# A fused attention and two-layer feed-forward kernel: layer 1 in three passes over 512 tokens

## The chip, the cores and the metric

The kernel runs on one core of one Trainium2 chip. The metric is device microseconds of one execution. The core's engines are named as in the profile: PE (TensorE, matmuls) and PEld (its weight loads), DVE (VectorE), ACT (ScalarE), POOL (GpSimd), SP (SyncE, which issues most DMAs); a q behind a name is that engine's sequencer.

## The reference, cut to what matters

```python
# q, k, v: (batch 2, heads 8, seq 768, 64); each query attends to the keys with its own 6-bit hash
q_bits = (q @ proj > 0); k_bits = (k @ proj > 0)         # bucket = the six bits
scores = where(q_bucket == k_bucket, q @ k.T / 8, -1e9)
attn = softmax(scores) @ v                               # -> x, 1536 tokens x 512
g = x @ w_gate                                           # layer 1: 512 -> 1536 -> 512
x = (g * sigmoid(g) * (x @ w_val)) @ w_out
h = x @ w_in                                             # layer 2: 512 -> 2048 -> 512
out = (max(h, 0) + alpha * min(h, 0)) @ w_out2
```

## The kernel before, in words

All matmul operands are split in two rounded parts, high and low, and each product is made of three matmuls (high by high, high by low, low by high; `mm3`). The engines' queues run in order; a scheduler lays the program out, and instructions that are pinned keep the program's order.

**Attention** goes item by item: 24 items, each a pair of heads and 256 queries, for batch 0 then 1, and per batch the 256-token groups in order with four pairs in each. An item has two units (heads); a unit makes three banks of scores, takes the maximum over the keys (VectorE, tiles `m`), broadcasts it by transposes, subtracts it (`se`, L303), takes the exponent and multiplies with the values (`po`, L315). K and Q come from DRAM; of K three copies are fetched at an item that is the first of its pair and batch: the two heads one above the other (`nat`), and side by side into the two halves of `kt` (L160, L161). The generator `attention` yields 16 times per item; the caller advances it with `more()`.

**Layer 1** has 12 feature blocks f of 128. For each, `gate` and `value` products (4 x 3 matmuls each) go into PSUM, then tanh (ScalarE), two gate steps (VectorE, L587 and L590), the high part (ScalarE) and the low part (GpSimd, L602); three blocks later (`D1`) the output product of the block is added into four accumulators that stay in PSUM (`Y`). `stage1(g)` does this for 256 tokens, where a PSUM bank holds two gate products of 256 columns; `stage1w` for 512. Groups 0 to 3 (tokens 0 to 1023) are run by `stage1`, woven with attention: after each `yield` of `stage1` the caller makes `RATES[g]` steps of attention. Group g starts when its four items are done, so four items run alone first. The last 512 tokens are run by `stage1w` after attention has ended.

**Weights** are blocks of 128 x 512, 36 for layer 1. They come as 64-bit words: a raw block is loaded (L488, two buffers), `round64` turns it into float32 (ACT L505, DVE L506 and L508, POOL L510), and it is split into the high part (ACT L545) and the low part (L552, by turns on GpSimd and VectorE) in a buffer `wb`, of which there are six. The first time a block is used its split form is also written to DRAM (`w`, L556); every later pass reloads it from there (L500). `w_ahead` says how many blocks ahead of the one in use loads, conversions and splits are issued (`LEAD`). Of layer 2's 32 blocks, 12 are converted beside groups 2 and 3 and parked in DRAM (`EARLY`, `whole`), 20 beside `stage1w` (`w_late`: two raw loads per feature block, issued on SP's queue ahead of the reloads).

**Layer 2** (`stage2`) runs three times over 512 tokens. X, layer 1's input and output, lies in SBUF whole (`xh`, `xl`), and is overwritten in place.

## Time and profile before

| | us |
|---|---|
| median of 3 runs (908.02 to 909.84) | 909.22 |
| the profiled execution, first to last instruction (its span) | 907.9 |
| PE busy by overlapping durations | 842.3 (93%) |
| DVE busy | 563.6 (62%) |
| ACT busy | 440.4 (49%) |
| POOL busy | 374.8 (41%) |

The profile is of one execution. Busy times are unions of durations, and matmul durations overlap, so PE's share overstates it; the time of a matmul in a full stream is the distance of starts. A share over the whole span mixes stages with different limits: the rows further below are therefore cut by stage.

### The profile page before, as it was taken

Reading aid. Unit: us, or ns where it says so; the run is one execution under the profiler, and the core shown is the slowest. Engines: PE = TensorE matmul, PEld = TensorE weight load, DVE = VectorE, ACT = ScalarE, POOL = GpSimd, SP = SyncE. Lnnn points to the kernel's source line nnn. Section 1 sums busy time; section 2 is a strip of 40 time slices with the busy share of each in tenths; the row PEclk is TensorE's granted clock in tenths of the full one; section 3 lists DMA queues with packets and bytes.
Section 4 is the critical chain, followed back from the end, with each engine's and each line's share of the span. In section 5 each row is a group of like instructions: output and inputs, shape, how many; then the busy total and the mean of one; then the engine's idle time right before and its main releaser. Section 6 shows DMA issues by size and latency. Waiting matters only on the chain.

```text
span 907.9 us, 13038 instructions
## 1 busy us (share of the span) xinstructions
PE 842.3 (93%) x4816; PEld 736.4 (81%) x4816; DVE 563.6 (62%) x856; ACT 440.4 (49%) x760; POOL 374.8 (41%) x327
## 2 busy tenths in 40 slices
PE   4797878777999999999999999899999999999998
PEld 3576776666899999999999987788888888888886
DVE  5699998978777657678786537563433343335332
ACT  5687565655655656565655323222433343333331
POOL 4214666665443312233221235454444444445442
PEclk8899998988999999999999999999999999999999
DMA  9324776788999756766766698998100010000001
GB/s 219 85 81 162 240 243 214 225 262 247 332 344 272 225 191 215 252 231 220 252 217 213 224 330 309 342 338 303 46 1 1 1 47 0 1 12 36 1 0 47
DMA packets 63487, 158.45 MB, mean 175 GB/s; under 512 B 18112, under 2 KB 24256, under 8 KB 63424
## 3 DMA queue, kind: packets, MB, share of 16 engines
q1 hardware_dynamic: 61264, 152.07, 50.6%
q0 software_dynamic: 2016, 5.51, 2.8%
q8 instruction: 38, 0.62, 0.3%
q14 instruction: 25, 0.20, 0.1%
q10 hardware_dynamic: 144, 0.05, 0.0%
HBM read 132.44 MB, written 25.17 MB: 174 GB/s over the span
## 4 chain that ended last, share of the span: by engine, by line
PE 67%; DVE 15%; DMA 4%; POOL 3%; issue 2%; ACT 2%; SPq 0%; DVEq 0%; POOLq 0%; ACTq 0%
PE po L315 9%; PE gp L607 5%; PE gp L609 5%; PE gp L608 5%; PE op L612 5%; PE hp L607 5%; PE hp L608 5%; PE op L613 5%; PE op L614 5%; PE hp L609 5%; PE yp L607 3%; PE yp L609 3%; PE yp L608 3%; DVE wt L508 2%; DMA raw<-in_wblk_dram 2%
## 5 line engine op out<-in xcount | busy, mean ns | idle before, releaser
L602 POOL TENSOR_TENSOR gl<-ex,gh 128x512 fp32r<-128x512 f32 (+1 forms) x108 | 117.1, 1084 | 293.2 <-ACT gh L599 242.6
L607 PE MATMUL gp<-xh,wb 128*128 128x256 f32 (+1 forms) x480 | 154.4, 322 | 11.9 <-ACT wb L545 5.9
L609 PE MATMUL gp<-xh,wb 128*128 128x256 f32 (+1 forms) x480 | 148.8, 310 | 6.9 <-POOL wb L552 5.5
L315 PE MATMUL po<-se,vv 128*128 128x256 f32 x576 | 146.2, 391 | 3.9 <-ACT se L308 3.3
L608 PE MATMUL gp<-xl,wb 128*128 128x256 f32 (+1 forms) x480 | 147.3, 307 | 2.6 <-POOL xl L344 2.6
L593 DVE TENSOR_SCALAR ex<-hp,al 128x512 f32<-128x512 f32 x48 | 36.0, 751 | 137.8 <-PE hp L609 137.8
L315 PEld LDWEIGHTS po<-se,vv 128*128 128x128 f32 x576 | 106.3, 197 | 17.8 <-ACT se L308 5.0
L599 ACT ACTIVATE gh<-ex 128x512 fp32r<-128x512 f32 (+1 forms) x108 | 57.8, 535 | 125.7 <-DVE ex L596 66.8
L545 ACT ACTIVATE wb<-w 128x512 fp32r<-128x512 f32 x96 | 60.6, 632 | 101.1 <-PE hp L609 79.2
L607 PEld LDWEIGHTS gp<-xh,wb 128*128 128x128 f32 x480 | 91.8, 191 | 21.7 <-ACT wb L545 9.0
L609 PEld LDWEIGHTS gp<-xh,wb 128*128 128x128 f32 x480 | 92.3, 192 | 13.1 <-POOL wb L552 7.1
L608 PEld LDWEIGHTS gp<-xl,wb 128*128 128x128 f32 x480 | 92.2, 192 | 7.1 <-POOL xl L344 2.8
L308 ACT ACTIVATE se<-se 128x1536 f32<-128x1536 f32 x48 | 71.3, 1485 | 51.8 <-DVE se L303 51.6
L303 DVE SCALAR_TENSOR_TENSOR se<-se,mb 128x1536 f32<-128x1536 f32 x48 | 83.8, 1745 | 7.8 <-PE mb L298 7.5
L278 ACT ACTIVATE se<-S 128x512 f32<-128x512 f32 x144 | 80.0, 594 | 17.4 <-PE S L277 16.0
L510 POOL TENSOR_TENSOR wt<-wt,wr 128x512 int32<-128x512 int32 x48 | 67.6, 1410 | 49.4 <-DVE wt L508 31.3
L276 PE MATMUL S<-QA,kt 128*128 128x256 f32 x288 | 81.1, 310 | 2.9 <-ACT se L278 1.4
L607 PE MATMUL yp<-gh,wb 128*128 128x256 f32 (+1 forms) x240 | 78.1, 327 | 4.2 <-ACT wb L545 4.1
L609 PE MATMUL yp<-gh,wb 128*128 128x256 f32 (+1 forms) x240 | 73.7, 313 | 4.5 <-POOL wb L552 4.5
L277 PE MATMUL S<-qb,kt 76*128 76x256 f32 x288 | 74.0, 288 | 2.2 <-ACT kt L199 2.1
L607 PE MATMUL hp<-xh,wb 128*128 128x512 f32 x192 | 74.7, 389 | 0.0
L608 PE MATMUL hp<-xl,wb 128*128 128x512 f32 x192 | 74.7, 389 | 0.0
(94 smaller groups left out, 1839.2 us busy)
## 6 DMA issues: line engine op xcount, KB each, us to landing
wb<-w SPq DMA_DIRECT2D x144, 512.0 KB, 4.6
raw<-in_wblk_dram SPq DMA_DIRECT2D x68, 512.0 KB, 4.4
w<-wb SPq DMA_DIRECT2D x36, 512.0 KB, 5.1
qr<-in_q_dram SPq DMA_DIRECT2D x24, 256.0 KB, 3.9
kt<-in_k_dram POOLq DMA_DIRECT2D x14, 384.0 KB, 9.4
nat<-in_k_dram SPq DMA_DIRECT2D x8, 384.0 KB, 6.8
vv<-in_v_dram SPq DMA_DIRECT2D x16, 192.0 KB, 7.0
whole<-wt SPq DMA_DIRECT2D x12, 256.0 KB, 2.2
```

Of the source, the lines that this page charges most:

```text
L276: nc.tensor.matmul(pt[:, i, :], lhsT=ka[:, sl], rhs=qa, start=True, stop=False)
L277: nc.tensor.matmul(pt[:, i, :], lhsT=kb[:, sl], rhs=qb, start=False, stop=True)
L278: nc.scalar.activation(out=u.se[:, 2 * j:2 * j + 2, :], in_=pt, func=AF.Copy)
L303: nc.vector.scalar_tensor_tensor(out=u.se, in0=u.se, scalar=FLOOR, in1=u.mx[:, None, :].to_broadcast([P, NC, GQ]), op0=ALU.max, op1=ALU.su ...
L308: nc.scalar.activation(out=u.se, in_=u.se, func=AF.Exp, scale=SCALE)
L315: nc.tensor.matmul(it.po[:, u.x, :], lhsT=VV[it.b, it.p][:, kb, u.x * D:u.x * D + P], rhs=u.se[:, kb, :], start=kb == 0, stop=kb == NC - 1)
L510: pin(nc.gpsimd.tensor_tensor(out=a, in0=a, in1=r, op=ALU.add))
L545: nc.scalar.activation(out=w_tile(i)[:, 0, :], in_=wt[i], func=AF.Copy)
L602: nc.gpsimd.tensor_tensor(out=l, in0=ex, in1=f32(h), op=ALU.subtract)
L607: nc.tensor.matmul(pt, lhsT=h, rhs=ah, start=first, stop=False)
L608: nc.tensor.matmul(pt, lhsT=h, rhs=al_, start=False, stop=False)
L609: nc.tensor.matmul(pt, lhsT=l, rhs=ah, start=False, stop=last)
```

## The change

Layer 1 runs three times over 512 tokens (chunks 0, 1, 2), all by the same generator. Chunk 0 starts when its eight items are done; chunks 0 and 1 are woven with attention at 1.9 steps per yield, chunk 2 runs alone with the late conversions. The output product is no longer accumulated over all blocks in PSUM: after blocks 0-3, 4-7 and 8-11 (`QF` = 4; issued one block later) a `quad` makes the four output blocks, each 12 matmuls into a bank of the gate products' tags, and copies or adds it to `acc` in SBUF. For this an output weight block holds 4 feature blocks of one output block, and its raw load reads four pieces. X is a ring of two chunks: chunk 0's result is written to DRAM and read back before its layer-2 pass, which is the last (order 1, 2, 0). `wb` has four buffers in layer 1 and six of its own in layer 2, with shorter leads in layer 1. K is fetched twice instead of three times; the second half of `kt` is copied by ScalarE. The prefetch of the first raw blocks begins at step 64 of attention, not 32; all 12 early blocks are converted beside chunk 1. The final low parts of chunks 0 and 1 are made by GpSimd.

```diff
-NGB = 2
-NEX = 3
+NG1 = 5
+NEX = (2, 3)
...
-WB = (3, 6)
-LEAD = (3, 4, 5, 7)
+WB = (3, 4, 6)
+LEAD = ((2, 2, 3, 5), (3, 4, 5, 7))
...
-D1 = 3
+QF = 4
...
-PRIME = (32, 6)
-RATES = (2.0, 2.4, 2.6, 2.6)
-EARLY = (0, 0, 6, 6)
+PRIME = (64, 6)
+RATES = (1.9, 1.9)
+EARLY = (0, 12)
+AHEAD = 6
...
-        return XG(it.b * NG + it.g, it.p)
+        c, i = divmod(it.b * NG + it.g, W // GQ)
+        return [t[:, it.p, i * GQ:(i + 1) * GQ] for t in chunk(c)]
...
-        nc.gpsimd.dma_start(out=KB(it)[0:D], in_=kview(it))
...
+    def copy_k(it, x):
+        nc.scalar.activation(out=KB(it)[0:D, x, :], in_=f32(KA(it))[0:D, x, :], func=AF.Copy)
...
+            todo += [lambda x=x: copy_k(it, x) for x in range(2)]
...
-        u.m1 = at.sm.tile([P, GQ], F32, tag="m1", name="m1", bufs=1)
+        u.m1 = m2[:, 0, :]
...
+    def quad_at(f):
+        return f // QF - 1 if f % QF == 0 and f else None
...
-        for f in range(F1 + D1):
-            if f < F1:
-                o += [2 * f, 2 * f + 1]
-            if f >= D1:
-                o.append(F1O + f - D1)
-        return o
+        for f in range(F1):
+            o += [2 * f, 2 * f + 1]
+            q = quad_at(f)
+            o += [] if q is None else range(F1O + q * KD, F1O + (q + 1) * KD)
+        return o + list(range(F2I - KD, F2I))
...
-    seq = order1() * (len(RATES) + 1) + o2 * NP2
+    seq = order1() * NP2 + o2 * NP2
     NWT = len(seq)
+    NW1 = NWT - len(o2) * NP2
...
-        ready[i] = wp.tile([P, 2, 512], F32R, tag="wb", name="wb", bufs=WB[1])
+        if i < NW1:
+            ready[i] = wp.tile([P, 2, 512], F32R, tag="wb", name="wb", bufs=WB[1])
+        else:
+            ready[i] = fin.pool.tile([P, 2, 512], F32R, tag="wb2", name="wb2", bufs=WB[2])
...
-        pin(nc.sync.dma_start(out=t, in_=wblk[w].bitcast(I32).rearrange("p (f t) -> p f t", t=2)))
+        if F1O <= w < F2I:
+            q, e = divmod(w - F1O, KD)
+            src = wblk[F1O + q * QF:F1O + (q + 1) * QF, :, e * P:(e + 1) * P].bitcast(I32)
+            pin(nc.sync.dma_start(out=t.rearrange("p (f c) t -> p f (c t)", f=QF),
+                                  in_=src.rearrange("f p c -> p f c")))
+        else:
+            pin(nc.sync.dma_start(out=t, in_=wblk[w].bitcast(I32).rearrange("p (f t) -> p f t", t=2)))
...
+        lead = LEAD[n >= NW1]
         for name, k, fn in (("load", 2, w_load), ("conv", 1, w_conv), ("h", 0, w_h)):
-            upto(name, n + LEAD[0] + k, fn)
-        upto("l", n + LEAD[0], w_l)
-        upto("h", n + LEAD[1], w_h)
+            upto(name, n + lead[0] + k, fn)
+        upto("l", n + lead[0], w_l)
+        upto("h", n + lead[1], w_h)
         upto("put", n + 1, w_put)
-        upto("conv", n + LEAD[2], w_conv)
-        while ws.load < min(NWT, n + (LEAD[3] if fresh[min(ws.load, NWT - 1)] else LEAD[2])):
+        upto("conv", n + lead[2], w_conv)
+        while ws.load < min(NWT, n + (lead[3] if fresh[min(ws.load, NWT - 1)] else lead[2])):
...
+    def gate_bank(tag):
+        return at.ps.tile([P, W], F32, tag=tag, name="gp", bufs=at.nb[tag])
+    def quad(q, acc, gs, xh, xl):
+        for e in range(KD):
+            h, l = flat(w_next())
+            yp = gate_bank("GY"[e % 2])
+            for i in range(QF):
+                sl = slice(i * P, (i + 1) * P)
+                mm3(yp, (h[:, sl], l[:, sl]), *gs[q * QF + i], i == 0, i == QF - 1)
+                if i == 1:
+                    yield
+            if q == 0:
+                nc.scalar.activation(out=acc[:, e, :], in_=yp, func=AF.Copy)
+            else:
+                nc.vector.tensor_tensor(out=acc[:, e, :], in0=yp, in1=acc[:, e, :], op=ALU.add)
+            if q == F1 // QF - 1:
+                nc.scalar.activation(out=xh[:, e, :], in_=acc[:, e, :], func=AF.Copy)
+                eng = nc.gpsimd if ws.busy else nc.vector
+                eng.tensor_tensor(out=xl[:, e, :], in0=acc[:, e, :], in1=f32(xh)[:, e, :], op=ALU.subtract)
+            yield
+    def stage1(c, conv=()):
+        xh, xl = chunk(c)
+        acc = at.lt.tile([P, KD, W], F32, tag="acc", name="acc", bufs=1)
...
+        conv = iter(conv)
...
+            ps = []
+            ex = tmp()
+            for tag in "GY":
+                pt = gate_bank(tag)
+                w = w_next()
+                for kk in range(KD):
+                    mm3(pt, (w[0][:, kk, :], w[1][:, kk, :]), xh[:, kk, :], xl[:, kk, :], kk == 0, kk == KD - 1)
+                    if kk == 1:
+                        yield
+                if tag == "G":
+                    gate_tanh(pt, ex)
+                    gate_mul(pt, ex)
+                    yield
+            gs[f] = g_tiles()
+            gate_val(pt, ex)
+            split_h(gs[f][0], ex)
+            split_l(gs[f][0], gs[f][1], ex)
+            yield
+            q = quad_at(f)
+            if q is not None:
+                yield from quad(q, acc, gs, xh, xl)
+        yield from quad(F1 // QF - 1, acc, gs, xh, xl)
...
         for i in range(W // P):
-            out_rows(t0 + i * P, ops[i], i, tmp())
+            out_rows(t0 + i * P, ops[i], i, fin.pool.tile([P, W], F32, tag="ob", name="ob", bufs=4))
...
-    X = [tx.tile([P, KD, B * S], F32R, name=n) for n in ("xh", "xl")]
+    CH = {}
+    def chunk(c):
+        if c not in CH:
+            CH[c] = [tx.tile([P, KD, W], F32R, tag=n, name=n, bufs=2) for n in ("xh", "xl")]
+        return CH[c]
...
-    while at.done < NPAIR:
-        at.alone = at.done < NPAIR - 2
+    per = NPAIR * (W // GQ)
+    while at.done < per:
+        at.alone = at.done < per - 2
...
-    for g, rate in enumerate(RATES):
-        while at.done < NPAIR * (g + 1):
-            more()
+    ws.busy = True
+    spill = dram.tile([2, P, KD * W], F32, name="spill")
+    for c, rate in enumerate(RATES):
         due = 0.0
         pre = 0.0
-        for _ in stage1(g):
-            pre += EARLY[g] / F1
+        over = 0
+        for _ in stage1(c):
+            pre += EARLY[c] / 20
...
-                more()
+                over += at.done >= per * (c + 2)
+                if over <= AHEAD:
+                    more()
+        while at.done < per * (c + 2):
+            more()
+        if c == 0:
+            for i, t in enumerate(chunk(0)):
+                nc.sync.dma_start(out=spill[i], in_=f32(t).rearrange("p k w -> p (k w)"))
...
-    stage1w(len(RATES) * GQ)
-    for n in range(NP2):
-        stage2(n * W)
+    ws.busy = False
+    for _ in stage1(2, w_late()):
+        pass
+    for n, c in enumerate((1, 2, 0)):
+        if n == 1:
+            CH.pop(0)
+            for i, t in enumerate(chunk(0)):
+                nc.sync.dma_start(out=f32(t).rearrange("p k w -> p (k w)"), in_=spill[i])
+        stage2(c)
```

Three places show how instructions move. On VectorE, in the stage that converts the 36 blocks, before (group 0; `raw` is a raw block, `m` a maximum, `ex<-ex,gp` a gate step):

```order
L506 TENSOR_SCALAR wt<-raw_1528 128x512
L552 TENSOR_TENSOR wb<-wt,wb 128x512
L508 SCALAR_TENSOR_TENSOR wt<-raw_1528,wt 128x512
L303 SCALAR_TENSOR_TENSOR se<-se,mb 128x1536
L506 TENSOR_SCALAR wt<-raw_1573 128x512
L285 TENSOR_TENSOR m_1922<-m_1919 128x256
L508 SCALAR_TENSOR_TENSOR wt<-raw_1573,wt 128x512
L506 TENSOR_SCALAR wt<-raw_1615 128x512
L587 SCALAR_TENSOR_TENSOR ex<-ex,gp 128x256
L508 SCALAR_TENSOR_TENSOR wt<-raw_1615,wt 128x512
L552 TENSOR_TENSOR wb<-wt,wb 128x512
L590 SCALAR_TENSOR_TENSOR ex<-ex,gp 128x256
```

In the changed kernel (chunk 0):

```order
L299 TENSOR_REDUCE mq<-mt 128x2
L571 TENSOR_TENSOR wb<-wt,wb 128x512
L198 TENSOR_SCALAR mk<-hp,ck 44x384
L288 TENSOR_TENSOR m_2421<-se 128x512
L525 TENSOR_SCALAR wt<-raw_2413 128x512
L309 SCALAR_TENSOR_TENSOR se<-se,mb 128x1536
L289 SCALAR_TENSOR_TENSOR m_2421<-se,m_2421 128x512
L527 SCALAR_TENSOR_TENSOR wt<-raw_2413,wt 128x512
L291 TENSOR_TENSOR m_2421<-m_2421 128x256
L607 SCALAR_TENSOR_TENSOR ex<-ex,gp 128x512
L198 TENSOR_SCALAR mk<-hp,cq 44x256
L525 TENSOR_SCALAR wt<-raw_2466 128x512
```

Before, the rounding steps of three blocks and one subtraction stand around the two gate steps of a feature block; now one block's steps and the first of another's, a whole maximum and a subtraction stand around a gate step of twice the width.

On PE, in the woven stage, before (`S` are scores, `mt` and `mb` the transposes of the maximum):

```order
L607 MATMUL yp<-gh,wb 128x256
L608 MATMUL yp<-gl,wb 128x256
L609 MATMUL yp<-gh,wb 128x256
L276 MATMUL S<-QA,kt_127 128x256
L277 MATMUL S<-qb_67,kt_127 128x256
L276 MATMUL S<-QA,kt_127 128x256
L277 MATMUL S<-qb_67,kt_127 128x256
L291 MATMUL mt<-ident,m_4127 128x128 x2
L298 MATMUL mb<-ident,mq 128x128 x2
L607 MATMUL gp<-xh,wb 128x256
L608 MATMUL gp<-xl,wb 128x256
L609 MATMUL gp<-xh,wb 128x256
```

In the changed kernel, in chunk 0:

```order
L282 MATMUL S<-QA,kt_124 128x256
L283 MATMUL S<-qb_66,kt_124 128x256
L627 MATMUL gp<-xh,wb 128x512
L628 MATMUL gp<-xl,wb 128x512
L629 MATMUL gp<-xh,wb 128x512
L627 MATMUL gp<-xh,wb 128x512
L628 MATMUL gp<-xl,wb 128x512
L629 MATMUL gp<-xh,wb 128x512
L297 MATMUL mt<-ident,m_3003 128x128 x2
L304 MATMUL mb<-ident,mq 128x128 x2
L627 MATMUL gp<-xh,wb 128x512
L628 MATMUL gp<-xl,wb 128x512
```

Attention's instructions are the same; the matmuls of layer 1 between them stream 512 columns, and stand in runs of six, as a yield follows two of the four k blocks.

On SP's queue, in the last pass of layer 1, where raw blocks of layer 2 are loaded beside reloads, before:

```order
L488 DMA raw_6119<-in_wblk_dram 128x1024
L488 DMA raw_6126<-in_wblk_dram 128x1024
L500 DMA wb<-w_83 128x1024
L500 DMA wb<-w_98 128x1024
L500 DMA wb<-w_84 128x1024
L488 DMA raw_6185<-in_wblk_dram 128x1024
L488 DMA raw_6192<-in_wblk_dram 128x1024
L500 DMA wb<-w_85 128x1024
L500 DMA wb<-w_99 128x1024
L500 DMA wb<-w_86 128x1024
```

In the changed kernel:

```order
L507 DMA raw_5024<-in_wblk_dram 128x1024
L507 DMA raw_5031<-in_wblk_dram 128x1024
L519 DMA wb<-w_86 128x1024
L519 DMA wb<-w_87 128x1024
L507 DMA raw_5076<-in_wblk_dram 128x1024
L507 DMA raw_5083<-in_wblk_dram 128x1024
L519 DMA wb<-w_88 128x1024
L519 DMA wb<-w_89 128x1024
L507 DMA raw_5128<-in_wblk_dram 128x1024
L507 DMA raw_5135<-in_wblk_dram 128x1024
```

Two raw loads are now followed by two reloads instead of three, while the output product's four reloads stand together elsewhere.

## Rows read from the trace of the kernel before

**Rows 1.** Busy time by stretch: engine busy us (instructions), PE clock, DMA share, GB/s.

```profile
0.00:86.00 86.00, 63.13 (x334) 49.59 (x334) 65.52 (x103) 59.06 (x101) 28.55 (x36) 0.92 0.54 129
86.00:239.50 153.50, 121.93 (x729) 106.12 (x730) 134.17 (x190) 89.85 (x161) 94.47 (x77) 0.91 0.78 250
239.50:540.60 301.10, 297.16 (x2173) 283.66 (x2171) 207.12 (x345) 168.27 (x302) 84.92 (x86) 1.00 0.75 245
540.60:642.70 102.10, 98.83 (x433) 80.94 (x434) 56.80 (x70) 31.69 (x52) 48.56 (x36) 1.00 0.86 312
642.70:907.90 265.20, 261.25 (x1153) 216.07 (x1151) 100.04 (x151) 91.50 (x147) 118.25 (x93) 1.00 0.03 13
```

**Rows 2.** Waits of PE, 86 to 239.5: us in total, times, longest.

```profile
PE gp L607 <- ACT wb L545: 5.9, 10, 0.9
PE gp L609 <- POOL wb L552: 5.5, 6, 1.6
```

**Rows 3.** Waits of all engines, 86 to 239.5.

```profile
ACT wb L545 <- POOL wt L510: 34.2, 21, 3.3
POOL wt L510 <- DVE wt L508: 23.8, 19, 3.7
```

**Rows 4.** Lines of DVE, 100.4 to 239.5: busy us, mean ns; idle before.

```profile
L508 DVE SCALAR_TENSOR_TENSOR wt<-raw,wt 128x512 int32<-128x512 int32 x30 | 27.1, 902 | 0.1
L506 DVE TENSOR_SCALAR wt<-raw 128x512 int32<-128x512 int32 x29 | 22.1, 763 | 1.3 <-DMA raw<-in_wblk_dram 1.3
L303 DVE SCALAR_TENSOR_TENSOR se<-se,mb 128x1536 f32<-128x1536 f32 x10 | 17.5, 1747 | 2.6 <-PE mb L298 2.5
L552 DVE TENSOR_TENSOR wb<-wt,wb 128x512 fp32r<-128x512 f32 x16 | 14.2, 885 | 7.6 <-ACT wb L545 7.4
L283 DVE SCALAR_TENSOR_TENSOR m<-se,m 128x512 f32<-128x512 f32 x9 | 9.8, 1091 | 0.2
L282 DVE TENSOR_TENSOR m<-se 128x512 f32<-128x512 f32 x9 | 8.5, 948 | 3.7 <-ACT se L278 3.7
L285 DVE TENSOR_TENSOR m<-m 128x256 f32<-128x256 f32 x10 | 7.1, 712 | 0.0
...
L590 DVE SCALAR_TENSOR_TENSOR ex<-ex,gp 128x256 f32<-128x256 f32 x12 | 4.9, 410 | 0.1
```

**Rows 5.** Single lines of DVE, whole span: ns min/median/max, first and last start.

```profile
L506 DVE TENSOR_SCALAR wt<-raw x48: 377/433/2337, 68.9 to 539.2; 128x512 int32<-128x512 int32 x48
...
L587 DVE SCALAR_TENSOR_TENSOR ex<-ex,gp x60: 402/421/689, 100.4 to 630.0; 128x256 f32<-128x256 f32 x48, 128x512 f32<-128x512 f32 x12
...
L282 DVE TENSOR_TENSOR m<-se x48: 648/692/1770, 17.1 to 497.1; 128x512 f32<-128x512 f32 x48
```

**Rows 6.** Timeline of PE, 256 columns: start us, duration us.

```profile
386.12 0.28 PE L607 MATMUL yp<-gh,wb 128*128 128x256 f32 x1
386.24 0.28 PE L608 MATMUL yp<-gl,wb 128*128 128x256 f32 x1
```

**Rows 7.** Timeline of PE, 512 columns.

```profile
700.25 0.39 PE L609 MATMUL hp<-xh,wb 128*128 128x512 f32 x1
700.47 0.39 PE L607 MATMUL hp<-xh,wb 128*128 128x512 f32 x1
```

**Rows 8.** Chain that ended last: start us, us; half an item's value products.

```profile
353.95 2.59 PE po L315 x12
```

**Rows 9.** Timeline of SP's queue, 540 to 578.

```profile
549.79 2.37 SPq L488 DMA_DIRECT2D raw<-in_wblk_dram  x2
...
555.34 2.78 SPq L488 DMA_DIRECT2D raw<-in_wblk_dram  x2
...
562.51 2.36 SPq L488 DMA_DIRECT2D raw<-in_wblk_dram  x2
```

**Rows 10.** Waits of PE, whole span.

```profile
PE gp L607 <- DMA wb<-w: 4.7, 3, 2.7
...
PE gp L607 <- DVE ex L590: 0.2, 1, 0.2
```

**Rows 11.** DMA issues, the page's part 6: KB each, median us to landing.

```profile
wb<-w SPq DMA_DIRECT2D x144, 512.0 KB, 4.6
```

More of the change, by code (lines that the diff above doesn't have):

```diff
@@ L624, in out_rows @@
         nc.sync.dma_start(out=out[r0:r0 + P, :], in_=ob)
-    gbank = []
-    def half_bank():
-        if not gbank:
-            t = at.ps.tile([P, 2, GQ], F32, tag="G", name="gp", bufs=2)
-            gbank.extend(((t[:, 1, :], 1), (t[:, 0, :], 0)))
-        return gbank.pop()
-    def full(w, xh, xl):
-        pt, n = half_bank()
-        for kk in range(KD):
-            mm3(pt, (w[0][:, kk, :], w[1][:, kk, :]), xh[:, kk, :], xl[:, kk, :], n == 0 and kk == 0,
-                n == 1 and kk == KD - 1)
-        return pt
@@ L726, in stage2 @@
                 ex = tmp()
-                gs[f] = [fin.pool.tile([P, W], F32R, tag=t, name=t, bufs=D2 + 1) for t in ("gh2", "gl2")]
+                gs[f] = g_tiles()
                 leak(hp, f, ex)
```

79 lines of the change are left out of this document (10 added, 69 removed).

## The prediction

> **What bounds the kernel now.** I began with the table of stretches [rows 1], cut where layer 1 changes its token group. Layer 2 (642.7 to the end) and the wide pass before it keep TensorE busy without a gap. So do groups 1 to 3 of layer 1, together 301.1 us with attention in between. Time is lost in two places: the first 86 us, where attention runs alone, and group 0 (86.0 to 239.5), where TensorE works 121.93 of 153.5 us by the overlapping durations, at a granted clock of 0.91 of 2.4 GHz. The waits of group 0 come next. TensorE waits for the high part of a weight from ScalarE and the low part from GpSimd [rows 2], and these wait further back in the conversion, ScalarE 34.2 us for GpSimd's rounding sum [rows 3], which itself follows VectorE's two rounding steps. VectorE is 134.17 us busy there, 87%: a group of 256 tokens has too little matmul work to lie beside the conversion of all 36 weight blocks.
>
> The lines of VectorE from the first gate multiply (100.4) to 239.5 show how full it is [rows 4, 5]. These rows sum to 111 us; the other gate step (5.0) and some 42 small operations at about 0.41 us bring it to some 133 of 139.1 us, 96%. A rounding step takes 0.763 us in the mean there, 0.433 in the median over the kernel, 2.337 at the longest [rows 4, 5].
>
> **TensorE's prices.** Only starts count, as durations overlap. In full streams a 256-column matmul starts 0.12 us after the last [rows 6], a 512-column one after 0.22 to 0.23 [rows 7], or 261.25 us / 1153 = 0.2266 in layer 2 [rows 1]. Two narrow ones cost 0.24, one wide 0.2266: 13.4 ns are saved per pair. The change turns 4 x 432 narrow matmuls into 2 x 432 wide ones: 864 x 13.4 ns = 11.6 us, where TensorE bounds. The Trainium skill has another price: "TensorE: Matmul & The Clock Gate", section Back-to-back issue gap, gives N/2.4 + 2.5 ns for an isolated stream, 109 and 216 ns, so 2.6 ns per pair and 2.2 us in all. The rows contradict it by 11 ns in each size. By the page the later overlapped pass below would be some 4.7 us shorter (432 x 11 ns), which I don't use.
>
> An attention item costs TensorE 24 score matmuls and 4 hash matmuls at 0.12, 24 value matmuls at 2.59/12 = 0.216 [rows 8] and 8 transposes at an estimated 0.1: 9.4 us. A pair's first item in a batch adds 8 hash matmuls of 384 columns, an estimated 1.4 us.
>
> **The change, stage by stage.**
>
> Start to the first gate multiply, 100.4 us now [rows 5]. By the order, VectorE's first conversion comes 29 rows later (four score maxima, four subtractions and what goes with them), and 75 rows instead of 39 stand between it and the first gate multiply, as eight items come first, not four. The 29 rows are 24 us at the means of rows 4 and 18 at undisturbed lengths (0.692 us for a maximum [rows 5]); I take 21. The 39 rows sum by rows 4 to 32.3 us and took 31.5 (68.9 to 100.4). The 75 rows sum to 62.8, times 31.5/32.3 = 61; with undisturbed maxima 54. Conversions are thinner there (7 in 75 rows against 6.5 in 39): 57. So 68.9 + 21 + 57 = 147 us, bounds 143 and 152. That three of the first ten K transfers are gone, and six ScalarE copies come in their place, I cost at nothing: ScalarE is busy 59.06 of the first 86 us [rows 1], so the copies have room; without it they cost six times some 0.8 us, the length of a copy of this shape by estimate, which the wider bounds hold.
>
> First pass over 512 tokens, to its end. TensorE needs 432 x 0.2266 = 97.9 us, 137 attention steps (72 yields x 1.9) = 8.5 items x 9.4 = 80, and 5.6 for four new pairs: 183 us. VectorE, counted in the order from the first gate multiply to the last accumulator add: 29 x (0.763 + 0.902) = 48.3 for roundings, 16 x 0.885 = 14.2 for low parts, 16 x 1.747 = 28.0 for subtractions, 16 x 0.948 + 16 x 1.091 + 15 x 0.712 = 43.3 for maxima, 24 wide gate steps at 0.69 (the longest narrow-or-wide one of rows 5) = 16.5, 8 adds of the same size = 5.5, 75 small ones = 30.8: 187 us, at 96% 195. The narrow matmul gain is thus hidden here, and so is the extra copying of the three-part output product on ScalarE (89.85 of 153.5 us busy). Bounds: 183 if TensorE decides, 195 by VectorE, 215 if the two, both near full, hold each other up by a tenth. I take 194, near VectorE's, since it is the engine that was full here before. Against 139.1 + 301.1 us for all four groups this is where the gain lies: the same 36 conversions are spread over a pass that has twice the matmuls, in place of a stage in which TensorE needed only some 98 of 153.5 us (432 x 0.12 + 4.9 items, by the order, x 9.4).
>
> Second pass: 97.9 + 7 items x 9.4 = 164 us for TensorE (the order leaves it 7 items). Groups 1 to 3 need 3 x 51.8 + 14.9 x 9.4 + 5.6 = 301 by the same prices and took 301.1, so 164 holds; 2 us are added for the last third of the output product, whose first matmuls wait for the last gate's low part: 166, up to 175 if writing chunk 0 out holds the ring's buffer. On SP's queue the two writes stand behind four reloads of the next pass; the fifth is queued behind them, and is wanted four blocks of some 4.5 us later.
>
> Third pass, alone, now 102.1 us: TensorE needs 97.9 as before. It now has 12 steps of two raw blocks, not 15, and a ring of four weight buffers, not six. While two raws and two reloads went out per step, SP's pairs of raw loads started 5.55 and 7.17 us apart [rows 9], 6.4 in the mean, against 24 x 0.227 = 5.4 us of matmuls; TensorE waited 4.7 us for reloads [rows 10]. Ten such steps now could lose 9.5 us, of which the two output parts, 10.9 us each without raws, give back some 6. I take 102, bounds 98 and 110.
>
> Layer 2 and the end: 265.2, unchanged; the reload of chunk 0 has a whole layer-2 pass in which to land. Halved reloads (144 to 72) are worth nothing of their own: the queues had room at a DMA share of 0.75 [rows 1].
>
> Sum: 147 + 194 + 166 + 102 + 265.2 = 874.2 us for the profiled execution, against its 907.9. The median of the runs before is 1.3 us above that span: 875.5.
>
> **Rivals.**
> 1. TensorE alone bounds the first pass: 183, and 143 to its start: 859 + 1.3 = 860 (for it: VectorE's rows are 153 us at undisturbed lengths, 0.433 us for the first rounding step and some 0.69 for the other wide ones; against it: GpSimd has the same 36 conversions to do beside them, and more wide splits).
> 2. The short ring starves the third pass: four buffers look 3 x 2.7 = 8 us ahead, a reload takes 4.6 us in the median [rows 11] and stands behind raw loads that wait for their buffers: 36 reloads lose a third of a us each, 12 us: 887. For it: the 4.7 us. Against: with three reloads per two raws nothing waited.
> 3. The first pass loses as much TensorE time as group 0 did (153.5 - 98 = 55 us), because the loss belongs to the chain of a weight and not to VectorE's load. TensorE would start 14 us before the first gate multiply, at 133, and end at 133 + 183 + 55 = 371 in place of 341: 905.5, no gain to speak of. For it: rows 2 and 3 name the chain. Against: a block is wanted every 5 us, no longer every 4.3.
> 4. Slower: PSUM banks. Each wide gate or output product takes a whole bank of only four, and most go back through VectorE, whose queue is then 95% full, with subtractions of 1.75 us ahead. 36 banks in the first pass, 1.5 us late each, would cost 54 us: 930. It decides from 0.95 us per bank (34/36). For it: the queue is in order. Against: TensorE waited 0.2 us for a gate step in the whole span [rows 10], and a bank has the whole of the other's product to come back in.
>
> **How the numbers follow.** Forecast 0.53, rival 1 0.20, rival 2 0.12, rival 3 0.06, rival 4 0.09. The time is the forecast's, 875.5. The range takes in rivals 1 in most and 2, and the upper bounds of the first pass and the second (21 and 9 us, not both whole): 855 to 903. A measurement of this kernel can tell about 0.2% (1.8 us) from no change. Rival 3 lies at that edge, half of it faster: faster 0.88, same 0.03, slower 0.09.
>
> **What would show it.** First gate multiply at 143 to 152; first pass over by 330 to 350, with TensorE's clock near 1.00 in it and VectorE about 90% busy; the second pass with TensorE busy throughout in some 166 us; 36 x 12 starts at 0.227 us in the third, some 102 us; layer 2 as before. I am wrong if the first pass takes over 225 us, with waits of TensorE for weight parts (rival 3) or for gate steps and adds (rival 4), or if reload waits in the third pass exceed 10 us.

## The result, and the profile after

The changed kernel takes 885.66 us in the median (882.12 to 886.66, 4 runs) where the kernel before takes 909.53 in the same session: a ratio of 0.9722, 95% interval 0.9691 to 0.9753. The forecast was 875.5 us. Its profiled execution spans 882.8 us, against 907.9.

The table of stretches, cut as in [rows 1], at TensorE's first gate matmul and the ends of the three passes over 512 tokens:

```profile
0.00:136.30 136.30, 106.07 (x558) 85.16 (x559) 110.69 (x173) 100.97 (x167) 43.30 (x46) 0.97 0.39 106
136.30:344.90 208.60, 193.32 (x974) 161.63 (x973) 179.39 (x260) 140.79 (x236) 113.72 (x89) 0.98 0.57 192
344.90:511.50 166.60, 166.04 (x840) 141.39 (x839) 108.33 (x167) 82.25 (x133) 49.76 (x40) 1.00 0.55 193
511.50:617.30 105.80, 100.90 (x434) 81.64 (x433) 58.68 (x76) 33.99 (x57) 48.81 (x37) 0.98 0.79 283
617.30:882.80 265.50, 261.40 (x1154) 216.12 (x1152) 102.47 (x152) 91.35 (x146) 118.19 (x93) 1.00 0.06 21
```

TensorE's row is full in the second pass and in layer 2. In the first pass and the third it is not, and the clock's mean is 0.98 there. VectorE's line of the first gate step says when the start was over (ns min/median/max, first and last start):

```profile
L607 DVE SCALAR_TENSOR_TENSOR ex<-ex,gp x36: 650/682/690, 148.8 to 603.8; 128x512 f32<-128x512 f32 x36
```

| | forecast, us | after, us |
|---|---|---|
| start to the first gate multiply | 147 | 148.8 |
| from there to the end of the first pass | 194 | 196.1 |
| second pass | 166 | 166.6 |
| third pass | 102 | 105.8 |
| layer 2 and the end | 265.2 | 265.5 |

For a closer look I measure the first pass from TensorE's first gate matmul to its last (136.3 to 345.0, 208.7 us), and hold against each pass the sum of its matmuls at the prediction's prices (0.2266 for 512 columns, 0.12 for 256, 0.216 for a value matmul, 0.175 for 384 columns, 0.109 for a transpose). What is above that sum I call lost. Before, group 0 lost 153.5 - 98.6 = 54.9 us and groups 1 to 3 lost 5.7 [rows 1]. After, the first pass lost 208.7 - 183.9 = 24.8 and the second 166.6 - 164.1 = 2.5. So 33 us less are lost. The sums themselves shrink by 46 us, since some four items more are done alone at the start and 512-column matmuls are cheaper; the start pays 50.3 us for that (86.0 to 136.3), the third pass 3.7. Together: 33 + 46 - 50 - 4 = 25 us, the difference of the spans.

What TensorE waited for in the first pass, 136 to 345 (us in total, times, longest):

```profile
PE mt L297 <- ACT se L284: 3.2, 2, 2.8
PE hp L192 <- ACT se L284: 2.8, 1, 2.8
PE S L283 <- ACT qb L204: 2.6, 1, 2.6
PE S L282 <- DVE se L309: 1.7, 2, 1.5
PE S L282 <- DVE mk L198: 1.6, 1, 1.6
PE mb L304 <- DVE mq L299: 1.5, 1, 1.5
...
```

The waits for weight parts of [rows 2] are gone. What is left are steps of attention that come late from ScalarE and VectorE, 15.1 us with the three short ones left out here. In group 0 all waits of TensorE came to 31.7 us.

Another part of the loss is TensorE's clock, which is granted at one of two levels, 1.00 (2.4 GHz) and 0.50 (1.2 GHz). In the changed kernel's third pass it fell after TensorE had stood idle for 2.44 us, and the 512-column matmuls then started 0.43 us apart (first the timeline of PE, then the stretch):

```profile
538.66 0.47 PE L627 MATMUL gp<-xh,wb 128*128 128x512 f32 x1 [2.44 <-DMA wb<-w]
...
539.26 0.63 PE L629 MATMUL gp<-xh,wb 128*128 128x512 f32 x1
539.69 0.63 PE L627 MATMUL gp<-xh,wb 128*128 128x512 f32 x1
```

```profile
539.10:542.50 3.40, 3.40 (x10) 2.62 (x9) 0.86 (x2) 0.00 (x0) 1.28 (x1) 0.50 1.01 399
```

By the mean clocks this costs at most (1 - 0.91) x 153.5 = 14 us in group 0 and (1 - 0.98) x 208.6 = 4 us in the first pass, an estimate that takes TensorE to be at work whenever its clock is low. So up to 10 of the 33 us are the clock's, beside the 16.6 us of waits that are gone.

### The profile page after: what moved, and what is told of

Same layout as the page of the kernel before. It is cut to its first block, busy times and chain, and to the rows that moved or that the text cites. A ratio compares the mean times of both kernels' runs of the same rounds, so it can differ in the third digit from the quotient of the medians.

```text
span 882.8 us, 11030 instructions
## 1 busy us (share of the span) xinstructions
PE 827.7 (94%) x3952; PEld 685.9 (78%) x3952; DVE 559.6 (63%) x824; ACT 449.3 (51%) x738; POOL 373.8 (42%) x304
## 4 chain that ended last, share of the span: by engine, by line
PE 69%; DVE 12%; ACT 7%; DMA 7%; issue 3%; POOL 1%; SPq 0%; DVEq 0%; ACTq 0%; POOLq 0%
PE po L321 9%; PE gp L628 7%; PE gp L629 7%; PE gp L627 7%; PE op L632 5%; PE hp L627 5%; PE hp L628 5%; PE op L633 5%; PE op L634 5%; PE hp L629 5%; PE S L283 2%; DMA raw<-in_wblk_dram 2%; PE S L282 2%; DMA wb<-w 2%; ACT se L314 2%
## 5 line engine op out<-in xcount | busy, mean ns | idle before, releaser
L622 POOL TENSOR_TENSOR gl<-ex,gh 128x512 fp32r<-128x512 f32 x84 | 111.7, 1330 | 182.8 <-ACT gh L619 182.6
L627 PE MATMUL gp<-xh,wb 128*128 128x512 f32 x288 | 122.4, 426 | 2.9 <-DMA wb<-w 2.9
L629 PE MATMUL gp<-xh,wb 128*128 128x512 f32 x288 | 114.7, 398 | 0.0
L628 PE MATMUL gp<-xl,wb 128*128 128x512 f32 x288 | 113.9, 396 | 0.1
L619 ACT ACTIVATE gh<-ex 128x512 fp32r<-128x512 f32 x84 | 53.0, 631 | 114.9 <-DVE ex L616 68.4
L529 POOL TENSOR_TENSOR wt<-wt,wr 128x512 int32<-128x512 int32 x48 | 65.5, 1368 | 100.3 <-DVE wt L527 56.5
L283 PE MATMUL S<-qb,kt 76*128 76x256 f32 x288 | 75.8, 292 | 3.4 <-ACT qb L204 2.6
L627 PE MATMUL hp<-xh,wb 128*128 128x512 f32 x192 | 74.7, 389 | 0.0
L629 PE MATMUL hp<-xh,wb 128*128 128x512 f32 x192 | 74.7, 389 | 0.0
L632 PE MATMUL op<-wb,gh 128*128 128x512 f32 x192 | 74.7, 389 | 0.0
L633 PE MATMUL op<-wb,gh 128*128 128x512 f32 x192 | 74.7, 389 | 0.0
L634 PE MATMUL op<-wb,gl 128*128 128x512 f32 x192 | 74.7, 389 | 0.0
L571 POOL TENSOR_TENSOR wb<-w,wb 128x512 fp32r<-128x512 f32 x48 | 61.9, 1289 | 24.1 <-ACT wb L564 24.1
```

The costliest lines, as they stand in the source:

```text
L283: nc.tensor.matmul(pt[:, i, :], lhsT=kb[:, sl], rhs=qb, start=False, stop=True)
L622: nc.gpsimd.tensor_tensor(out=l, in0=ex, in1=f32(h), op=ALU.subtract)
L627: nc.tensor.matmul(pt, lhsT=h, rhs=ah, start=first, stop=False)
L628: nc.tensor.matmul(pt, lhsT=h, rhs=al_, start=False, stop=False)
L629: nc.tensor.matmul(pt, lhsT=l, rhs=ah, start=False, stop=last)
L632: nc.tensor.matmul(pt, lhsT=gh, rhs=h, start=first, stop=False)
```

## The experiments

Stretches are from the table of stretches of each profiled run. "Lost" is the first pass less its sum, as above. Kernels whose edits take no work from VectorE or GpSimd in the first pass and give them none (spread, narrow, more transfers, K three times) lose 20 to 27 us in it: so far does this number move by itself. The waits of TensorE in that pass move less, 13.5 to 16.5 us in these kernels, so they tell more. The first gate matmul of kernels whose edits leave the start alone (these and "two VectorE steps more") stands at 132.5 to 139.3.

| kernel | first gate matmul | first pass | lost | TensorE's waits in it | VectorE / GpSimd busy in it | second | third | median, us | ratio to before (95%) |
|---|---|---|---|---|---|---|---|---|---|
| changed | 136.3 | 208.7 | 25 | 15.1 | 179 / 114 | 166.6 | 105.8 | 885.66 | 0.9722 (0.9691 to 0.9753) |
| late loads spread | 135.9 | 209.0 | 25 | 15.0 | 179 / 114 | 166.6 | 98.9 | 877.58 | 0.9634 (0.9600 to 0.9668) |
| narrow matmuls | 139.3 | 209.4 | 20 | 13.9 | 172 / 117 | 170.5 | 114.9 | 896.27 | 0.9832 (0.9787 to 0.9878) |
| low parts on GpSimd | 130.1 | 217.9 | 33 | 23.3 | 177 / 133 | 166.6 | 108.7 | 891.47 | 0.9784 (0.9735 to 0.9833) |
| low parts on VectorE, spread | 130.9 | 213.7 | 30 | 20.6 | 193 / 93 | 166.7 | 99.0 | 877.36 | 0.9624 (0.9600 to 0.9648) |
| two VectorE steps more | 132.5 | 221.8 | 38 | 25.0 | 196 / 114 | 168.6 | 107.6 | 899.66 | 0.9866 (0.9845 to 0.9887) |
| one rounding step less | 127.9 | 211.3 | 27 | 15.5 | 163 / 114 | 166.6 | 106.6 | 880.16 | 0.9645 (0.9604 to 0.9685) |
| smaller maximum | 119.2 | 207.1 | 25 | 15.7 | 153 / 113 | 166.6 | 106.3 | 869.29 | 0.9541 (0.9508 to 0.9575) |
| no GpSimd sum | 131.4 | 204.0 | 20 | 13.2 | 174 / 72 | 166.6 | 106.4 | 875.29 | 0.9647 (0.9572 to 0.9721) |
| no rounding at all | 128.5 | 195.6 | 14 | 6.3 | 139 / 73 | 166.6 | 107.0 | 864.36 | 0.9461 (0.9430 to 0.9492) |
| more transfers | 136.8 | 211.3 | 27 | 16.5 | 180 / 113 | 166.5 | 107.4 | 887.70 | 0.9751 (0.9720 to 0.9782) |
| K three times | 137.8 | 204.4 | 20 | 13.5 | 181 / 121 | 166.6 | 106.4 | 883.76 | 0.9701 (0.9660 to 0.9741) |

### The third pass: late raw loads spread

```diff
+        ws.due += ws.rate          # in w_next, once per weight block
+        while ws.due >= 1.0:
+            ws.due -= 1.0
+            next(ws.late, 0)
...
-            for _ in range(-(-(len(late) + RAWB) // F1)):
-                next(conv, 0)
...
+    ws.late = w_late()
+    ws.rate = 0.65
```

> The changed kernel with the raw loads and conversions of the last layer-2 weights spread evenly over all 36 weight blocks of the third pass, 0.65 of a step per block, in place of two steps together before each of the first feature blocks. Theory, that the third pass loses its 7.9 us above 36 x 12 x 0.2266 = 97.9 us because pairs of raw loads stand together ahead of reloads: the pass falls from 105.8 to about 100, the time by 4 to 6 us, to about 880. Rival, that a ring of four weight buffers is too short for a reload wherever the raw loads stand: the pass stays at 104 to 107 and the time within 2 us. Second rival, that steps which now reach into the blocks of the output product move the loss there or past the end of the pass: 107 to 110.

The third pass fell to 98.9 us, 1 us above its 97.9, and the median by 8 us, more than the 4 to 6 expected. In the changed kernel, SP's queue in that pass starts the raw loads by twos, and reloads behind them:

```profile
519.16 3.35 SPq L507 DMA_DIRECT2D raw<-in_wblk_dram  x2
522.61 0.86 SPq L519 DMA_DIRECT2D wb<-w  x2
524.77 3.33 SPq L507 DMA_DIRECT2D raw<-in_wblk_dram  x2
528.20 0.38 SPq L519 DMA_DIRECT2D wb<-w  x1
531.87 2.35 SPq L507 DMA_DIRECT2D raw<-in_wblk_dram  x2
```

and TensorE waits in it, 511.6 to 617.3, for the reloads:

```profile
PE gp L627 <- DMA wb<-w: 4.3, 4, 2.4
```

With the steps spread, its queue starts them one by one among the reloads:

```profile
512.13 0.37 SPq L508 DMA_DIRECT2D raw<-in_wblk_dram  x1
514.41 3.04 SPq L520 DMA_DIRECT2D wb<-w  x2
517.55 0.38 SPq L508 DMA_DIRECT2D raw<-in_wblk_dram  x1
519.85 3.04 SPq L520 DMA_DIRECT2D wb<-w  x2
```

and TensorE no longer waits for a reload. The pass's row in the table of stretches has the clock at 1.00 and much the same data (31 MB, where it was 30) in less time:

```profile
511.50:610.40 98.90, 98.19 (x433) 81.00 (x432) 49.30 (x75) 33.68 (x57) 49.11 (x37) 1.00 0.87 314
```

A pair of raw loads holds the queue for 2.4 to 3.4 us in these lines, as the second waits for its buffer, and the reloads wait behind it. The waits of SP's queue in the changed kernel, 511.6 to 617.3, say how long in all:

```profile
SPq L507 <- DVE w L527: 30.1, 16, 3.0
```

A ring of four buffers is long enough when no pair stands in front; the order was at fault. Of the 6.9 us won, 4.3 are the waits; the eight matmuls at the lower clock behind the longest of them, some 0.2 us longer each, are an estimated 1.6 more. This version beats both kernels.

### The price of a wide matmul

```diff
-                    mm3(pt, ...)
+                    mm3n(pt, ...)   # each matmul as two of 256 columns; also in quad
```

> The changed kernel with every layer-1 matmul of 512 columns (gate, value and output product) issued as two of 256 columns, in the same banks and order; nothing else differs. Theory, that a narrow pair costs 13.4 ns more than a wide matmul, as the starts in the rows of the kernel before say: 432 pairs are 5.8 us in each pass that TensorE bounds, so second pass 166.6 to about 172, third pass 105.8 to about 111; the first pass hides it behind VectorE, 0 to 3 us; together 11 to 15 us slower, about 898. Rival, that a pair costs only 2.6 ns more, the price that I worked out in the prediction from the Trainium skill's page TensorE: Matmul & The Clock Gate, section Back-to-back issue gap, and from no row of this case: 1.1 us in each of these passes, together 2 to 3 us slower, about 888.

The stretches of the second and the third pass with narrow matmuls:

```profile
348.70:519.20 170.50, 170.06 (x1273) 164.54 (x1272) 107.61 (x167) 82.61 (x133) 49.99 (x40) 1.00 0.53 189
519.20:634.10 114.90, 107.86 (x867) 106.97 (x866) 59.57 (x78) 35.08 (x58) 48.49 (x37) 0.97 0.75 261
```

The second pass is 3.9 us longer, between the two prices: 9 ns per pair. The third is 9.1 longer, but there TensorE also waits more for reloads (6.6 us in place of 4.3) at a lower clock, so it prices nothing. The starts tell why it is 9 and not 13. The timeline of PE in the changed kernel's second pass (start us, duration us):

```profile
400.32 0.39 PE L628 MATMUL gp<-gl,wb 128*128 128x512 f32 x1
400.55 0.39 PE L629 MATMUL gp<-gh,wb 128*128 128x512 f32 x1
400.78 0.40 PE L627 MATMUL gp<-gh,wb 128*128 128x512 f32 x1
401.02 0.39 PE L628 MATMUL gp<-gl,wb 128*128 128x512 f32 x1
```

They are 0.23 to 0.24 apart, 231 ns in the median of that pass. In the third pass of the spread kernel it is 227:

```profile
560.23 0.39 PE L634 MATMUL gp<-xh,wb 128*128 128x512 f32 x1
560.46 0.39 PE L632 MATMUL gp<-xh,wb 128*128 128x512 f32 x1
560.68 0.39 PE L633 MATMUL gp<-xl,wb 128*128 128x512 f32 x1
```

Narrow ones are 120 ns apart in both passes. So by the starts a pair gains 13 ns where layer 1 runs alone, and 9 beside attention. In the first pass the narrow form costs 0.7 us, less than that pass moves by itself. The median is 10.6 us higher, just short of the 11 to 15 of the theory.

### What bounds the first pass

Four edits take work from VectorE or GpSimd, three add or move it.

```diff
-        nc.vector.scalar_tensor_tensor(out=a, in0=t[:, :, 1], ...)   # round64, layer 1 only
```

> The changed kernel without the second of VectorE's two rounding steps for the layer-1 weights, so that this part of the conversion is left out. It takes 29 x 0.785 = 22.8 us from VectorE in the first pass and shortens each weight's chain by one step. Theory, that VectorE's load alone holds the first pass above TensorE's need: 196 falls to TensorE's 183 to 186, the first gate multiply comes 3 to 5 us earlier (7 fewer roundings ahead of it), and the time falls by 13 to 18 us to about 870. Rival, that the pass waits for something else (attention's own chain of maximum, subtraction and exponential, or GpSimd): the pass falls by less than 5 us. The second and the third pass stay as they are in both.

The pass did not get shorter, with 17 us less on VectorE:

```profile
127.90:339.20 211.30, 195.42 (x983) 163.00 (x982) 162.60 (x233) 140.55 (x238) 114.37 (x89) 0.97 0.57 189
```

Nor did it from the first gate multiply (140.6), 198.6 us where it was 196.1. The whole gain, some 6 us, came ahead of it: the first gate matmul stands 8.4 us earlier. The theory falls.

```diff
-        nc.vector.tensor_tensor(out=m2, ...)          # 512 columns
-        nc.vector.scalar_tensor_tensor(out=m2, ...)   # 512 columns
+        nc.vector.tensor_tensor(out=u.m1, in0=u.se[:, 0, :], in1=u.se[:, 5, :], op=ALU.max)
...
-        nc.scalar.activation(out=u.se, in_=u.se, func=AF.Exp, scale=SCALE)
+        nc.scalar.activation(out=u.se, in_=u.se, func=AF.Exp, scale=0.0)
```

> The changed kernel with a smaller maximum in attention: one VectorE step of 256 columns over two of the six score blocks in place of two of 512 and one of 256 over all, and an exponential of a constant, so that the softmax is not the reference's; the conversion of the weights stays whole. In the first pass it takes 18 x (1.22 + 0.83) = 37 us from VectorE and 2 us from the chain of each half item. There TensorE loses 25 of 208.7 us from its first gate matmul; without the rounding of the weights it lost 14. Theory, that VectorE's queue is what TensorE meets late, whatever fills it: the loss falls to 10 us or less, the pass to 185 to 194. Rival, that the loss hangs on the conversion's chain through GpSimd, whose parts for VectorE are unchanged here: the pass stays at 203 or more. In both TensorE's first gate matmul comes 10 to 30 us earlier, since VectorE is the fullest engine before it, 110.7 of 136.3 us.

The start is 17 us shorter, the pass is not:

```profile
0.00:119.20 119.20, 97.97 (x566) 82.65 (x567) 84.00 (x139) 99.65 (x165) 39.98 (x45) 0.97 0.44 121
119.20:326.30 207.10, 191.46 (x967) 161.02 (x966) 152.85 (x223) 141.29 (x238) 113.03 (x91) 0.97 0.58 193
```

So VectorE's part sets the length of the start: 27 us less of it make it 17 us shorter. Whether by its load or by its place in attention's chain, both of which the edit shortens, this run does not say. In the first pass VectorE can be a quarter idle, and TensorE loses the same 25 us and waits as long. The waits of VectorE show where the freed time goes, first in the changed kernel's first pass, then in this one's:

```profile
DVE wt L525 <- POOL wb L571: 8.2, 4, 3.7
```

```profile
DVE wt L523 <- POOL wb L569: 13.0, 9, 3.7
```

VectorE's first rounding step writes a buffer `wt` that GpSimd's low part of an earlier weight must have read. With less work, VectorE waits longer there; without the second rounding step it waits 10.1 us.

```diff
+        if not full:      # layer 1 only
+            nc.scalar.activation(out=a, in_=t.bitcast(U32)[:, :, 0], func=AF.Copy, ...)
+            return
```

> The changed kernel without the rounding of the layer-1 weights: VectorE's two steps and GpSimd's sum are left out, and ScalarE's step writes the weight directly, so that part of the conversion is missing; raw loads, high parts, low parts and writes stay. It takes 29 x (0.64 + 0.78) = 41 us from VectorE and 29 x 1.40 = 41 us from GpSimd in the first pass and leaves a weight's chain one short step. From TensorE's first gate matmul to the end the pass took 208.7 us, and the starts of its matmuls at undisturbed spacing sum to 184. Theory A, that those 25 lost us belong to the conversion, by load or by chain: the pass falls to 184 to 190. Theory B, that they belong to attention's own chain of copies, maxima, transposes and exponentials, which TensorE meets in order: it stays at 200 or more. In both the first gate multiply comes some 10 us earlier.

The loss falls to 14 us, between the two theories, and TensorE's waits to 6.3 us, all for ScalarE's copies of the scores (the stretch of the pass, then its waits):

```profile
128.50:324.10 195.60, 189.23 (x966) 159.75 (x965) 139.09 (x198) 139.58 (x235) 72.96 (x59) 0.97 0.61 202
```

```profile
PE mt L297 <- ACT se L284: 4.8, 2, 3.3
PE mb L304 <- ACT se L284: 0.9, 1, 0.9
PE S L282 <- ACT se L284: 0.6, 1, 0.6
```

So some 11 of the 25 us belong to the rounding as a whole, and 14 remain without it. VectorE no longer waits for GpSimd here.

```diff
-        pin(nc.gpsimd.tensor_tensor(out=a, in0=a, in1=r, op=ALU.add))   # layer 1 only
```

> The changed kernel without GpSimd's sum in the rounding of the layer-1 weights, so that this part of the conversion is left out; VectorE's two steps stay. It takes 30 x 1.40 = 42 us from GpSimd in the first pass and one step of 1.4 us from a weight's chain. Theory, that GpSimd's step (its length in the chain, or the lengthening of VectorE's steps while GpSimd runs) is what the kernel without any rounding won by: the loss of 25 us falls to 14 to 18, the pass from 208.7 to 198 to 202. Rival, that it was VectorE's share of the rounding: the loss stays at 22 or more, the pass at 206 to 210.

204.0 us with 20 lost lies between, and no further off than the kernel with K three times, whose edit takes nothing from the pass. TensorE's waits, 13.2 us, are no shorter than there either, so this run tells nothing apart. One of its four executions took 886.09 us where the others took 874 to 875, hence its wide interval. Neither the sum alone nor VectorE's second step alone shortens TensorE's waits, then, while the whole rounding is worth 9 us of them.

```diff
-            eng = nc.gpsimd if i % n < m else nc.vector
+            eng = nc.gpsimd if i < NW1 or i % n < m else nc.vector
```

> The changed kernel with the low parts of all 36 weight blocks of layer 1 on GpSimd, where every second one was on VectorE. It takes 16 x 0.85 = 13.6 us from VectorE in the first pass and puts 16 x 1.35 = 21.6 us on GpSimd, which is busy 140.79 of 208.6 us there. Theory, that VectorE's load sets the length of the first pass: it falls by 8 to 13 us, from 196 to 183 to 188 between the first gate multiply and the end, and the time to about 875. Rival, that it is the length of a weight's chain over the engines (GpSimd's sum and difference follow VectorE's roundings), or the two engines together: no gain, or 2 to 8 us slower. The other passes do not change in either.

From the first gate matmul the pass is 9.2 us longer instead of shorter, from the first gate multiply 7.6: the rival's sign and size. VectorE waits 18.4 us for GpSimd's low parts, where it was 8.2, and the median is 891.47 us, not about 875. The opposite, on top of the spread steps:

```diff
+            eng = nc.gpsimd if i >= NW1 and i % n < m else nc.vector
```

> The kernel with the spread steps of the third pass (877.6 us), and all low parts of the layer-1 weights on VectorE, where every second one was on GpSimd: 18 x 0.89 = 16 us more on VectorE, 16 x 1.36 = 22 us less on GpSimd in the first pass. Theory, that VectorE's load holds the pass: 8 to 14 us longer, about 888. Rival, that GpSimd's slow part of a weight's chain holds it, since the opposite move made the pass 8 us longer and less load on VectorE alone did not make it shorter: 3 to 8 us shorter, about 872. Between them, that it belongs to attention: within 3 us.

Its pass begins 5 us earlier and is 4.7 us longer than that of the spread kernel, with the same end (344.6 and 344.9) and the same time. From the first gate multiply the two passes differ by 0.3 us (196.8 and 196.5), which is what was expected if the pass belongs to attention. That does not show that it does: TensorE's waits grew to 20.6 us, so this move, like the other, makes attention's steps later, and the half and half split is the best of the three.

```diff
+            if ws.busy:       # behind each feature block
+                for _ in range(2):
+                    nc.vector.tensor_scalar(out=ex, in0=ex, scalar1=0.0, scalar2=al[:, 0:1], ...)
```

> The changed kernel with two more VectorE steps of 512 columns behind each feature block of the first two passes, on a tile that nobody reads again: 24 x 0.68 = 16 us per pass. Theory, that VectorE's load sets the first pass: it grows by 12 to 16 us, and the second, where VectorE is busy 108 of 166.6 us, by 0 to 2. Rival, that VectorE has room in the first pass, too, and only the order of what waits matters: both grow by less than 4 us.

```profile
132.50:354.30 221.80, 196.75 (x974) 162.26 (x973) 196.00 (x282) 140.34 (x236) 114.31 (x89) 0.97 0.54 180
354.30:522.90 168.60, 166.33 (x839) 141.38 (x838) 117.48 (x191) 82.57 (x133) 49.42 (x40) 1.00 0.54 191
```

The first pass takes 13 us more, the second 2.0, as VectorE's load would have it. But the added steps write `ex`, which GpSimd's low part of the gate product still reads, so they add waits of VectorE, too. In the first pass these are

```profile
DVE ex L697 <- POOL gl L622: 5.7, 6, 2.3
```

and in the second 16.0 us. So the 13 us cannot be put down to load alone. Load taken away from VectorE alone gives nothing there (two runs), and a bound by VectorE's sum does not behave so. Queues in order could, when TensorE, too, meets attention's steps in a fixed order: each step is late by what stands ahead of it on its own engine, GpSimd's low parts among it. That is my reading; no run tests it by itself.

### Group 0 of the kernel before

The same omission in the kernel before (the second rounding step, layer 1 only):

> The kernel before without the second of VectorE's two rounding steps for the layer-1 weights, so that this part of the conversion is left out. Group 0 took 139.1 us from the first gate multiply, of which VectorE's rows filled 133. Theory of the prediction, that VectorE's load sets group 0: 29 x 0.90 = 26 us less, group 0 at 113 to 118, the time at about 880. Rival, that the chain of a weight over ScalarE, VectorE and GpSimd sets it: one step of five shorter, group 0 falls by 3 to 12 us. Groups 1 to 3 stay at 301 in both.

Group 0 took 139.5 us from TensorE's first gate matmul, and its matmuls 103.3 by the prices; the loss fell from 54.9 to 36 us. From the first gate multiply it fell by 11.7, the rival's figure, and the median is 890.79 us (ratio 0.9767, 0.9740 to 0.9794), not about 880. The stretch, and TensorE's waits for weight parts, which go on, 86 to 226:

```profile
86.30:225.80 139.50, 115.93 (x764) 103.34 (x763) 112.79 (x165) 94.23 (x167) 93.63 (x80) 0.96 0.83 268
```

```profile
PE gp L608 <- ACT wb L546: 5.8, 6, 2.0
PE gp L610 <- POOL wb L553: 3.5, 5, 1.0
...
```

VectorE is 112.8 us busy there, 81%. Of the 19 us, TensorE's waits gave 8 (31.7 to 23.5), and its clock, 0.96 in place of 0.91, at most 8 more. VectorE's second step was a part of what held group 0, by its load or by its place in a weight's chain; the rest of that chain still holds it.

### The transfers

```diff
+            if i < 2 * F2I:
+                nc.sync.dma_start(out=twin[w], in_=scratch[w])
```

> The changed kernel with 36 further transfers of 512 KB in the second pass, each behind a reload on the same queue, from where the reload reads to a place that nobody reads. It doubles the reads of that pass, so that it carries more than the passes of the kernel before did. Theory, that the reloads that the change saves are worth nothing, since the queues had room: the second pass stays at 166 to 168, the time within 2 us of 885.7. Rival, that fewer reloads are part of the gain: TensorE waits for weight buffers and the second pass takes 175 or more. If the starts of the wide matmuls in that pass, 231 ns apart in the median where they are 227 in the third, belong to the transfers, they go to 235 or more.

The transfers did not go where I wanted them: the scheduler put them into the first pass. There the DMA share rose from 0.57 to 0.79 and the pass by 2.6 us; the second pass carried no more than before:

```profile
136.80:348.10 211.30, 194.44 (x975) 161.43 (x974) 180.06 (x260) 140.13 (x236) 113.28 (x89) 0.98 0.79 271
348.10:514.60 166.50, 165.94 (x839) 141.35 (x838) 107.97 (x167) 82.25 (x133) 49.79 (x40) 1.00 0.54 190
```

That is no more than this pass moves by itself, so a load of 271 GB/s is harmless there. For the second it was not tested, and what makes its matmuls start 231 ns apart stays open.

```diff
+        nc.gpsimd.dma_start(out=KB(it)[0:D], in_=kview(it))
...
-            todo += [lambda x=x: copy_k(it, x) for x in range(2)]
```

> The changed kernel with K fetched three times again, as before: a third transfer per pair through GpSimd's queue in place of ScalarE's two copies. Theory of the prediction, that this part is worth nothing, since ScalarE has room and so have the queues: the first gate multiply at 147 to 151, the end of the first pass at 343 to 347, the time within 2 us of 885.7. Rival, that the copies hold ScalarE up where attention alone runs (ScalarE is busy 101 of 136.3 us there, six copies of 0.73 us are 4.4) or in the first pass: the first gate multiply 3 to 5 us earlier, or the loss of 25 us in the pass smaller by 3 or more. Second rival, that the transfers themselves were late: the first gate multiply later than 152.

First gate multiply at 151.1, end of the first pass at 342.2, the time 1.9 us lower in the median with overlapping intervals: nothing that can be told from no change. ScalarE's copies take 0.83 us each in the changed kernel, as the prediction's 0.8 had it and not the 0.73 of this expectation.

## Why the prediction was right, and where its steps were off

The stretch from the first gate multiply to the end of the first pass, as the prediction cut it:

```profile
148.80:344.90 196.10, 180.91 (x915) 151.80 (x914) 167.30 (x243) 131.53 (x222) 109.71 (x85) 0.97 0.58 196
```

1. **Start.** 148.8 for 147, inside the bounds. That VectorE's part sets it, as the counting of its rows assumed, is shown by the smaller maximum: the first gate multiply came 18 us earlier. With the rounding step left out it came 8 us earlier, which says less, as it lies between 145.0 and 151.8 in kernels whose start is untouched. K was rightly costed at nothing.
2. **First pass.** The size was right (196.1 for 194), the reason was not. The step that failed is "I take 194, near VectorE's, since it is the engine that was full here before". VectorE was to be busy 187 of 195 us, 96%. In that stretch it was busy 167 of 196, 85%; with 153 us of 207 the pass is as long. The sum of rows was 20 us too large, in part since the lengths of group 0 did not carry over (the rounding steps took 0.640 and 0.781 us, not 0.763 and 0.902), and the idle time 20 us too small: the two cancelled, and that is luck. I also began TensorE's 183 us at the first gate multiply, though its matmuls begin 12.5 us before that, so the true loss was 25 us and not 11. In place of a full VectorE the runs show TensorE waiting 15 us for attention's steps and a few us at the lower clock. The clock was to be near 1.00 and was 0.98. Rival 1 (TensorE alone) falls with the same rows, though VectorE's load alone does not hold it up.
3. **Rivals 3 and 4.** No wait for a weight part, a gate step or an add is left in the first pass; 25 us are lost and not 55 or more. That VectorE's load alone made the loss of group 0 was too much: 30 us of it taken away (33 steps of 0.9) gave 19 us less loss, and TensorE still waits 23.5 us there.
4. **Second pass.** 166.6 for 166. The count by rows held. The prediction also has the price N/2.4 + 2.5 ns of the Trainium skill's page "TensorE: Matmul & The Clock Gate", section Back-to-back issue gap, which the page gives for the isolated gap of single matmuls, not for a kernel's stream. By that price the pass would have been an estimated 4.7 us shorter. This trace does not agree: the starts are 231 ns apart, not 216.
5. **Third pass.** 102 was 3.8 us short, the largest miss of a term. The waits that I feared there came (4.3 us, and some 1.6 more at the lower clock behind the longest), but rival 2's 12 us did not, and its cause was another: the ring is long enough, and the pairs of raw loads on the queue were in the way. I had this row in hand and gave back 6 us for the output parts that did not come back.
6. **The price of 13.4 ns a pair** holds where layer 1 runs alone; beside attention it is 9. Of 11.6 us some 4 us are shown as a gain, in the second pass. In the first, where they were predicted to be hidden, the 0.7 us found are too few to tell from none.

The sum of the terms missed by 8.6 us, of which 3.8 is the third pass; the median stands 2.9 us above the span, where 1.3 were taken.

**Still open:** which queue makes attention's steps late in the first pass, and how much the buffers `wt`, through which VectorE waits for GpSimd, have to do with it: a kernel with more of them was not tried. No run spreads the conversions without the rest of the change, so that this spreading is what ended the waits for weight parts is argued from the rows before and after, not shown by itself. The rounding as a whole is worth 11 of 25 us. Kernels with the same first pass differ by up to 5 us in it, so smaller parts could not be told apart. More raw buffers, which would test the loads ahead of ScalarE's first step, were not tried.

## What to carry to other kernels

Here a stage that converts data beside too little matmul work got cheaper when the same conversions lay beside twice the matmuls (33 us less lost), and the loss to compare is TensorE's time above its matmuls' own prices, not the fullest engine's busy share. VectorE, at 86% the fullest engine beside TensorE in the first pass, looked like the bound, and 17 or 27 us less of its work left that pass as long: test a claimed bound by taking work away. When you add work instead, see what the added steps wait for, or the run tests their waits, too. When a ring of buffers is shortened, first look at what stands between its loads on the queue: spreading the other loads took the ratio from 0.9722 to 0.9634 here, 8 us, without a further buffer.
